# Residues of sums moved into the last attention round, a first reciprocal in two parts, and a reordered second stage, in a causal attention with a PReLU MLP behind it

## The chip, the cores and the metric

One core of one Trainium2 chip. The metric is the device time of one execution in microseconds; each kernel is timed in several runs and the median counts. "Before" has a median of 625.0 us over three runs (623.92 to 625.7).

## The reference

```python
# attention: 4 batches x 12 heads, 448 rows, 64 wide
scores = (1 / sqrt(64)) * q @ k.T                # causal mask: -1e9 above the diagonal
scores = scores - max(scores, axis=-1)
attn = exp(scores); attn = attn / (sum(attn, axis=-1) + 1e-9)
attn_out = attn @ v
x = attn_out.transpose(0, 2, 1, 3).reshape(1792, 768)
# MLP: w_in is 768 x 2048, w_out is 2048 x 768, alpha has 2048 entries
h = x @ w_in
g = maximum(h, 0) + alpha * minimum(h, 0)
out = g @ w_out
```

The MLP's weights arrive as 64-bit numbers, of which the kernel builds 32-bit ones itself.

## The kernel before, in words

**Attention.** Two heads make a pair; there are 24 pairs in 28 rounds (0 to 27). The loop `attention` runs through ORDER, a list written out by hand, once in each round; an entry such as `PT1+3` does step PT1 for the pair of three rounds ago. The letters: LK and LQ load k and q, S0, S1, S2 (SF for the first and last pair) make scores on TensorE, MX takes row maxima on VectorE, EX exponentials with their sums on ACT, RC the reciprocal of the seven sums on VectorE, NO normalizes p (on POOL; the letter behind the lag names the engine), PT transposes p on TensorE, C copies the transposes from PSUM (a is ACT, d VectorE), AV multiplies by v, XH/XN/XF/XL split the result into a rounded high part and a low part, ST stores the low parts to DRAM, LV loads chunks of v as LOADV says. Round 2 has a list of its own, SECOND_ROUND. The order of this text is the order of each engine's queue; nothing reorders it.

**Sums and residues.** The MLP's first product is done by a scheme that needs sums of the attention's results (T1 to T4, for two halves of the tokens and two column blocks: 16 in all). They lie in `spare`, the memory that later holds the accumulator acc1. Each sum becomes a rounded part (`t_hi`, line 399 on ACT or 403 on POOL) and a residue (`t_lo`, line 574), which is put into the list `late` and stored by a later `flush`. An entry `T` of the table EARLY does one sum on POOL; `th` and `tl` in the table FIRST do it on ACT and VectorE.

**Weight pieces.** A piece of the weights is loaded (LD), A (its absolute value, ACT), C (clamp, POOL), four operations D on VectorE (lines 253, 257, 260, 261), + (addition on POOL), and then cast (rounding, ACT) and sub (residue, POOL). EARLY, FRONT and REAR say in which round which piece is at which step; in a round they run at the entries ED, E2 and EA, one D at EG.

**Behind the attention.** `h_plain` makes the first group's products h = x @ w_in (24 of them, six matmuls each; 14 run inside the last rounds), with high parts from SBUF and low parts loaded back from DRAM (`load_low`, line 668, four buffers). `h_act` is the PReLU, `g_hi` and `g_lo` its rounded part and residue (lines 747, 752), `o_half` a half of a row block of the output product (six matmuls, line 786), whose bank ACT evicts for the first group (line 792). There are eight PSUM banks: four hold the h of the second token block (q = 1) until `h_act` has read it, the others and those that come free take the o halves in turn. The steps 0 to 28 of FIRST run beside these products: steps 1 to 10 behind one h product each, step 11 and later behind one o half each. In one step the kinds run in the order of KINDS: act, gh, gl, D, load, abs, cast, tl, st, th, add, S, sub, clamp. From then on four more groups follow in cycles that the change doesn't touch.

Queues: SP issues nearly all transfers and runs them in program order; a load whose data is still being stored waits there, with all behind it.

Of the kernel before, what the change touches and what calls it, by code (L numbers as in the profile page):

```python
# [24 lines left out]
EARLY = {  # L25
# [5 lines left out]
}  # L31
# [5 lines left out]
E2+4 LK+0 LQ+0 LT+4 NO00+3p NO10+3p MX11+2 NO21+3p NO11+3p EX10+2 EX11+2 MX20+2 NO20+3p MX21+2 EX20+2 NO30+3p MX00+2 EX00+2 AV+4 S2+2 LV+4 PT1+3 PT0+3 PT2+3 EX21+2 MX01+2 EX01+2 XF+4 XN+4 XH+4 C10+3a MX30+2 EG+4 XL+4 EX30+2 C00+3d C21+3d RC+2 ED+4 NO01+2p C20+3a PT3+3 S0+1 S1+1 SF+1 C30+3a EA+4 MX10+1 ST+4  # L37
# [19 lines left out]
14: D.i3.1.2 load S.S3.1 cast.A11.1  # L57
15: tl cast.S2.1
16: gh.1X gl.1X add.i3.1 sub.A11.1
17: gh.1W gl.1W cast.S3.1 sub.S2.1 S.S4.1 th  # L60
18: sub.S3.1 abs.o0.1 cast.A12.1
19: tl clamp.o0.1 sub.A12.1
20: D.o0.1.2 th
21: D.o0.1.2
22: tl add.o0.1 st load
23: gh.1Z gl.1Z abs.o1.1
24: clamp.o1.1
25: D.o1.1.1
26: D.o1.1.1
# [51 lines left out]
def kernel(  # L121
# [14 lines left out]
    nc = tc.nc  # L136
# [316 lines left out]

    def row_rec(p):
        sm, r = T["sm", p], ap["b2"].tile([P, 2 * NQ + 1], F32, tag="rs", name=f"rs_{p}")
        T["r", p] = r
        nc.vector.tensor_tensor(out=sm, in0=sm, in1=least, op=ALU.add)
        nc.vector.reciprocal(r, sm)
# [417 lines left out]
    def plan_early():  # L876
# [40 lines left out]
    low_calls = {1: 1, 2: 1, 3: 1, 4: 1, 5: 1, 7: 1, 8: 1, 9: 1, 11: 1}  # L917

    with tc.manual_schedule():
# [175 lines left out]
```

## Time and profile before

| | before |
|---|---|
| median of three runs | 625.0 us |
| profiled execution | 625.2 us |
| its span | 623.4 us |
| TensorE busy | 609.2 us (98%) |
| VectorE, POOL, ACT busy | 498.9, 397.8, 282.7 us |
| mean granted TensorE clock | 0.994 |
| attention, without its last product, until | about 171.7 us |
| second group starts | about 216 us |

The span is the time from the first to the last instruction; the execution's own time is 1.8 us longer. A granted clock of 1.00 is 2.4 GHz and 0.50 is 1.2 GHz. TensorE is busy nearly all the time, so its idle places and the places with a lower clock are where time can come from; idle time of the others costs nothing by itself. Names such as t_W are program tiles (W is one of the four blocks X, Y, Z, W of h); `<-` in brackets names the instruction that ended a wait.

### The profile page before, as it was taken

How to read it: one execution, taken by the hardware profiler on the slowest of the kernel's cores; microseconds unless marked ns; L12 is line 12 of the kernel's file. 1: busy time of each engine (PE TensorE's matmuls, PEld its weight loads, DVE VectorE, ACT ScalarE, POOL GpSimd, SP SyncE). 2: the span in 40 equal slices, each digit the busy share in tenths (PEclk: the TensorE clock that was granted, in tenths of full speed). 3: DMA queues.
4: the chain of work that ended last, by engine and by line, in shares of the span. 5: the costliest groups of instructions: out<-in, count | busy, mean ns of one | idle time of the engine just before them, and what ended most of it. 6: DMA issues, size and time to landing. Idle time of an engine off the chain costs nothing.

```text
span 623.4 us, 10906 instructions
## 1 busy us (share of the span) xinstructions
PE 609.2 (98%) x3527; PEld 532.7 (85%) x3527; DVE 498.9 (80%) x1115; ACT 282.7 (45%) x778; POOL 397.8 (64%) x531
## 2 busy tenths in 40 slices
PE   7989999999997999999999999999999999999997
PEld 4666666666877999999999999989999999999997
DVE  5889999999479678797798779868977987796364
ACT  6978989897455654232332323232333323231210
POOL 5655778767596568865776686567667766772130
PEclk9999999999998999999999999999999999999999
DMA  8674487634757479566756765685667667554725
GB/s 180 173 193 126 149 227 211 196 119 120 236 199 264 135 216 307 172 212 198 237 180 192 224 215 155 204 258 172 194 211 224 181 206 225 176 178 135 246 82 197
DMA packets 88329, 120.40 MB, mean 193 GB/s; under 512 B 12272, under 2 KB 66304, under 8 KB 88272
## 3 DMA queue, kind: packets, MB, share of 16 engines
q1 hardware_dynamic: 87664, 118.46, 61.9%
q0 software_dynamic: 288, 0.79, 0.6%
q8 instruction: 28, 0.46, 0.3%
q10 hardware_dynamic: 320, 0.46, 0.3%
q14 instruction: 29, 0.24, 0.1%
HBM read 105.00 MB, written 14.68 MB: 192 GB/s over the span
## 4 chain that ended last, share of the span: by engine, by line
PE 89%; DVE 4%; DMA 2%; POOL 1%; ACT 1%; issue 1%; SPq 1%; POOLq 0%; DVEq 0%; ACTq 0%
PE o L786 37%; PE heldY L688 11%; PE heldX L688 8%; PE a L496 6%; PE pt L477 6%; PE heldZ L688 5%; PE s L422 5%; PE s L414 3%; PE heldW L688 3%; PE h_V L688 3%; DVE s L434 1%; ACT p L449 1%; DMA low_N<-low_N 1%; DMA lo_N<-low_N 1%; PE warm L342 1%
## 5 line engine op out<-in xcount | busy, mean ns | idle before, releaser
L794 DVE TENSOR_TENSOR acc<-o,acc 128x384 f32<-128x384 f32 x196 | 107.4, 551 | 77.2 <-PE o L786 76.3
L403 POOL TENSOR_SCALAR p<-p,rs 128x128 f32<-128x128 f32 (+3 forms) x164 | 80.4, 511 | 46.6 <-ACT ptf L399 28.0
L449 ACT ACTIVATE p<-s,nm 128x256 f32<-128x256 f32 (+3 forms) x168 | 81.9, 497 | 16.1 <-DVE nm L434 15.6
L786 PE MATMUL o<-wo,g_Z 128*128 128x384 f32 x336 | 79.1, 344 | 4.2 <-DVE t_W L738 4.2
L786 PE MATMUL o<-wo,g_W 128*128 128x384 f32 x336 | 78.4, 340 | 0.3 <-POOL g_W L752 0.3
L786 PE MATMUL o<-wo,g_X 128*128 128x384 f32 x336 | 77.5, 338 | 0.0
L434 DVE CUSTOM_DVE_ANT_0 s<-s,mask 128x256 f32<-128x256 f32 (+3 forms) x168 | 70.9, 479 | 7.9 <-PE s L422 5.3
L786 PE MATMUL o<-wo,g_Y 128*128 128x384 f32 x336 | 76.9, 336 | 0.0
L786 PEld LDWEIGHTS o<-wo,g_Z 128*128 128x128 f32 x336 | 61.8, 191 | 7.6 <-ACT wi_A L291 4.5
L786 PEld LDWEIGHTS o<-wo,g_X 128*128 128x128 f32 x336 | 60.7, 188 | 3.2
L786 PEld LDWEIGHTS o<-wo,g_W 128*128 128x128 f32 x336 | 61.7, 191 | 0.6 <-POOL g_W L752 0.6
L786 PEld LDWEIGHTS o<-wo,g_Y 128*128 128x128 f32 x336 | 60.6, 188 | 0.0
L496 PEld LDWEIGHTS a<-ptf,v 128*64 128x64 f32 x384 | 25.3, 136 | 33.3 <-issue 11.8
L477 PEld LDWEIGHTS pt<-ident,p 128*128 128x128 f32 x384 | 43.1, 141 | 11.8 <-issue 7.9
L264 POOL TENSOR_TENSOR y_i<-y_i,x_i 128x384 f32<-128x384 f32 x32 | 33.5, 1047 | 27.1 <-DVE x_i L261 27.1
L496 PE MATMUL a<-ptf,v 128*64 128x448 f32 (+3 forms) x384 | 47.0, 386 | 2.2 <-DMA v<-in_v_dram 1.7
L477 PE MATMUL pt<-ident,p 128*128 128x128 f32 x384 | 47.0, 274 | 1.1 <-POOL p L403 0.7
L264 POOL TENSOR_TENSOR y_o<-y_o,x_o 128x384 f32<-128x384 f32 x32 | 32.8, 1024 | 22.4 <-DVE x_o L261 20.6
L399 ACT ACTIVATE ptf<-pt 128x512 f32<-128x512 f32 (+1 forms) x72 | 38.2, 575 | 6.5 <-PE pt L477 6.4
L247 ACT ACTIVATE x_i<-raw_i 128x384 f32<-128x384 f32 x32 | 17.8, 557 | 46.4 <-DMA raw_i<-in_moe_w_in_dram 46.4
L422 PE MATMUL s<-kr,qr 64*128 64x256 f32 (+2 forms) x288 | 38.6, 395 | 0.0
L752 POOL TENSOR_TENSOR g_Z<-t_Z,g_Z 128x384 fp32r<-128x384 f32 (+1 forms) x15 | 18.5, 1232 | 31.4 <-ACT g_Z L747 31.4
(188 smaller groups left out, 1347.0 us busy)
## 6 DMA issues: line engine op xcount, KB each, us to landing
lo_T<-low_T SPq DMA_DIRECT2D x28, 512.0 KB, 4.6
lo_B<-low_B SPq DMA_DIRECT2D x25, 512.0 KB, 4.6
raw_i<-in_moe_w_in_dram SPq DMA_DIRECT2D x32, 384.0 KB, 3.6
raw_o<-in_moe_w_out_dram SPq DMA_DIRECT2D x32, 384.0 KB, 3.6
lo_T<-low_T SPq DMA_DIRECT2D x28, 384.0 KB, 3.7
lo_B<-low_B SPq DMA_DIRECT2D x25, 384.0 KB, 3.9
lo_N<-low_N SPq DMA_DIRECT2D x16, 512.0 KB, 4.9
lo_N<-low_N SPq DMA_DIRECT2D x16, 384.0 KB, 4.6
```

Source lines behind the costliest of these rows:

```text
L264: nc.gpsimd.tensor_tensor(out=y, in0=y, in1=xf, op=ALU.add)
L399: eng.activation(out, x, AF.Copy, scale=side)
L403: eng.tensor_scalar(out=out, in0=x, scalar1=side, scalar2=1.0, op0=ALU.mult, op1=ALU.mult)
L414: nc.tensor.matmul(ps, qd[p % 3], T["k", p], start=True, stop=True)
L422: nc.tensor.matmul(ps[:, o : o + lim], T["q", p][half(j), i * QP : (i + 1) * QP], T["k", p][half(j), :lim], start=(o == 0), stop=(n > 0 or ...
L434: nc.vector.tensor_tensor_reduce(out=t, in0=t, in1=masks[1] if i == NQ else masks[0][:, (NQ - 1 - i) * QP :], scale=-SCALE, scalar=MOST_F3 ...
L449: nc.scalar.activation(T["p", p, i][:, j, : t.shape[1]], t, AF.Exp, scale=-1.0, bias=T.pop(("nm", p, i, j)), accum_out=T["sm", p][:, z : z ...
L477: nc.tensor.transpose(ps[:, j - js[0], c], t[:, j, c * QP : (c + 1) * QP], T["ident"])
L496: nc.tensor.matmul(out[half(j), c * QP :], vs[b % 2][:, hp, c, j], x[:, c * QP : S], start=(c == 0), stop=(c == NQ),)
L688: nc.tensor.matmul(ps, w[:, u, k * P : (k + 1) * P], x, start=(first and i == 0), stop=(i == len(mms) - 1), skip_group_check=True,)
L786: nc.tensor.matmul(ps[:, :NH], x, w, start=(i == 0), stop=(i == 3 * GC - 1))
L794: nc.vector.tensor_tensor(out=a[:, cols], in0=ps[:, :NH], in1=a[:, cols], op=ALU.add)
```

## The change

- EARLY: the steps of the weight pieces in rounds 5 to 19 are spread differently; what stood in round 26 goes to a new table MID, run at a new entry EH of ORDER, in front of the copies of the last transposes. In it stand seven `U`, each a sum whose rounded part is made on ACT and whose residue on VectorE, instead of four `T` on POOL. In round 26 the copy C10 goes behind EH.
- FIRST: only four sums are left there (steps 20 to 27), a flush `st` at step 0 stores the seven residues, and several steps move: h_act of block W from step 11 to 9 and of Z from 11 to 10, two of the third piece's D operations behind them, and the casts of the sums S1 to S3 one to three steps later.
- Rounds 2 and 3 have lists of their own (ROUNDS): the reciprocal of the first pair is made in two parts (RA for four sums, RB for three), its normalizations and two of its transposes move into round 2, one normalization goes to VectorE.
- `row_norm`: VectorE is used where the list asks for it, and for block 1 of the last pair alone (before: of the first and the last).
- LOADV: rounds 4 to 7 load 3, 2, 2, 0 chunks of v instead of 2, 2, 2, 1.
- Half of the first pair's q is loaded by POOL's queue instead of SP's; the memset for the warming products comes before three others.

```diff
 EARLY = {
-    5: "A:0", 6: "C:0 D:0:1", 7: "D:0:2 A:1", 8: "C:1", 12: "D:0:1 LD D:1:1 T",
-    13: "+:0 D:1:2 A:2 cast:A21", 14: "D:1:1 C:2 LD D:2:1", 15: "D:2:2 +:1 A:3 T",
-    16: "D:2:1 C:3 sub:A21 LD D:3:1 cast:A22", 17: "D:3:1 T", 18: "D:3:1 +:2 sub:A22 cast:L1", 19: "D:3:1 LD T",
+    5: "A:0", 6: "C:0 D:0:2", 7: "A:1 D:0:2", 8: "LD C:1 +:0", 9: "D:1:1 A:2", 10: "C:2", 11: "D:2:1",
+    12: "T D:1:1", 13: "D:1:2 LD cast:A21", 14: "+:1 A:3 D:2:1", 15: "D:2:1 T C:3", 16: "sub:A21 D:2:1 LD cast:A22",
+    17: "D:3:2 T", 18: "D:3:1 +:2 sub:A22 cast:L1", 19: "T D:3:1 LD",
     20: "+:3 cast:A11", 21: "sub:L1 cast:A12", 22: "sub:A11 cast:L0 A:4", 23: "sub:A12 C:4 A:5", 24: "sub:L0 C:5",
-    25: "LD +:4 T D:5:4 LD", 26: "C:6 C:7 D:6:4 LD T T +:6 T T",
+    25: "LD +:4 T D:5:4 LD", 
 }
 FRONT = {25: "D:4:4", 26: "+:5 A:6 A:7"}
+MID = {26: "C:6 C:7 U U U D:6:4 LD U U U U +:6"}
 REAR = {26: "D:7:4 LD +:7"}
-LOADV = {0: 2, 1: 2, 2: 2, 3: 1, 9: 4, 10: 3, 12: 2, 13: 3, 14: 2}
+LOADV = {0: 3, 1: 2, 2: 2, 9: 4, 10: 3, 12: 2, 13: 3, 14: 2}
...
-... C10+3a MX30+2 EG+4 XL+4 EX30+2 C00+3d C21+3d RC+2 ED+4 ...
+... C10+3a MX30+2 EG+4 XL+4 EX30+2 EH+4 C00+3d C21+3d RC+2 ED+4 ...
-SECOND_ROUND = """
-LK+0 LQ+0 MX11+2 EX10+2 EX11+2 MX20+2 MX21+2 EX20+2 MX00+2 EX00+2 EX21+2 MX01+2 EX01+2 MX30+2 S0+1 S1+1 SF+1 MX10+1 MX11+1 EX30+2 RC+2 NO01+2p
-"""
+ROUNDS = {2: """
+LK+0 LQ+0 MX11+2 EX10+2 EX11+2 MX00+2 EX00+2 MX01+2 EX01+2 MX20+2 EX20+2 MX21+2 EX21+2 RA+2 NO10+2p NO11+2p NO00+2p NO01+2p MX30+2 S0+1 S1+1 PT1+2 PT0+2 MX10+1 MX11+1 EX30+2 RB+2 NO20+2p NO21+2d NO30+2p
+""", 3: """
+LK+0 LQ+0 EX10+2 EX11+2 MX00+2 EX00+2 MX01+2 EX01+2 MX20+2 S2+2 EX20+2 MX21+2 PT2+3 EX21+2 C10+3a C00+3d MX30+2 EX30+2 C21+3d RC+2 NO01+2p C20+3a PT3+3 S0+1 S1+1 SF+1 C30+3a MX10+1
+"""}
 FIRST = """
-0: ... cast.o0.0 cast.o1.0
-1: ... cast.o2.0 cast.o3.0 th
-2: ... sub.o2.0 tl
-3: D.i1.1.2 add.i0.1 sub.o3.0 th
-4: D.i1.1.2 load tl
-5: act.1Y act.1X add.i1.1 th
-6: gh.1Y tl abs.i2.1
+0: ... cast.o0.0 cast.o1.0 st
+1: ... cast.o2.0 cast.o3.0
+2: ... sub.o2.0
+3: D.i1.1.2 add.i0.1 sub.o3.0
+4: D.i1.1.2 load
+5: act.1Y act.1X add.i1.1
+6: gh.1Y abs.i2.1
 7: gl.1Y clamp.i2.1 S.S1.1
-8: D.i2.1.2 cast.S1.1 th
-9: D.i2.1.2 load sub.S1.1 cast.L1.1
-10: add.i2.1 sub.L1.1 tl abs.i3.1
-11: act.1W act.1Z clamp.i3.1
-12: S.S2.1 cast.A22.1 th
-13: D.i3.1.2 sub.A22.1
+8: D.i2.1.2
+9: act.1W D.i2.1.1
+10: act.1Z cast.S1.1
+11: D.i2.1.1 load sub.S1.1 cast.L1.1
+12: add.i2.1 abs.i3.1 sub.L1.1
+13: clamp.i3.1 S.S2.1
...
     def load_first():
-        load(0, "q")
+        load(0, "q", also=nc.gpsimd)
...
+    def row_rec(p, cols=slice(0, 2 * NQ + 1)):
+        sm = T["sm", p]
+        if ("r", p) not in T:
+            T["r", p] = ap["b2"].tile([P, 2 * NQ + 1], F32, tag="rs", name=f"rs_{p}")
+        nc.vector.tensor_tensor(out=sm[:, cols], in0=sm[:, cols], in1=least[:, cols], op=ALU.add)
+        nc.vector.reciprocal(T["r", p][:, cols], sm[:, cols])
...
-        if p in edge and i == 1:
+        if eng is nc.vector or p == edge[1] and i == 1:
...
+        first[26] = order_of(ORDER.replace("C10+3a ", "").replace("EH+4 ", "EH+4 C10+3a "))
...
+                    elif kind == "U":
+                        fns.append(lambda: (t_hi(nc.scalar), t_lo(nc.vector)))
```

## Rows read from the trace of the kernel before

**Rows 1.** What TensorE waited for: us in total, times, longest us.

```profile
PE o L786 <- DVE t_W L738: 4.2, 1, 4.2
...
PE a L496 <- DMA v<-in_v_dram: 1.7, 1, 1.7
```

**Rows 2.** Windows of 2 us: busy us (x instructions) by engine, clock, DMA share, GB/s.

```profile
196.00:198.00 2.00, 0.00 (x0) 0.00 (x0) 1.97 (x5) 2.00 (x7) 1.83 (x3) 0.65 0.56 146
...
202.00:204.00 2.00, 2.00 (x10) 2.00 (x9) 2.00 (x2) 2.00 (x7) 2.00 (x3) 0.65 0.62 111
```

**Rows 3.** Order of time on TensorE: start us, us, instruction [idle before <-releaser].

```profile
171.74 1.95 PE L496 MATMUL a<-ptf,v 128*64 128x448 f32 x16
...
198.16 1.30 PE L786 MATMUL o<-wo,g_Z 128*128 128x384 f32 x3 [4.18 <-DVE t_W L738]
...
200.22 1.16 PE L786 MATMUL o<-wo,g_Z 128*128 128x384 f32 x3
...
201.18 1.16 PE L786 MATMUL o<-wo,g_W 128*128 128x384 f32 x3
...
204.30 0.68 PE L786 MATMUL o<-wo,g_W 128*128 128x384 f32 x3
...
204.82 0.68 PE L786 MATMUL o<-wo,g_Z 128*128 128x384 f32 x3
```

**Rows 4.** Order of time on VectorE, 165 to 199 us.

```profile
165.70 0.42 DVE L401 COPY ptf<-pt 128x256 f32<-128x256 f32 x1 [5.83 <-PE pt L477]
...
179.16 0.56 DVE L738 SCALAR_TENSOR_TENSOR t_Z<-h_Z,t_Z 128x384 f32<-128x384 f32 x1 [3.25 <-ACT t_Z L735]
...
184.38 1.44 DVE L574 TENSOR_TENSOR acc<-acc,xw 128x448 fp32r<-128x448 f32 x1
...
195.14 0.36 DVE L260 TENSOR_SCALAR x_i<-y_i 128x384 int32<-128x384 int32 x1
...
195.53 0.56 DVE L261 SCALAR_TENSOR_TENSOR x_i<-raw_i,x_i 128x384 f32<-128x384 uint32 x1
...
197.32 0.69 DVE L738 SCALAR_TENSOR_TENSOR t_W<-h_W,t_W 128x512 f32<-128x512 f32 x1
```

**Rows 5.** Residue instructions by line: ns min/median/max, first and last start us.

```profile
L574 POOL TENSOR_TENSOR acc<-acc,xw x9: 1135/1154/1330, 70.7 to 174.8; 128x448 fp32r<-128x448 f32 x9
L574 DVE TENSOR_TENSOR acc<-acc,xw x7: 612/618/1441, 184.4 to 209.8; 128x448 fp32r<-128x448 f32 x7
...
L399 ACT ACTIVATE xw<-acc x7: 560/564/570, 180.2 to 205.4; 128x448 fp32r<-128x448 f32 x7
...
L403 POOL TENSOR_SCALAR xw<-acc x9: 558/567/877, 70.1 to 173.8; 128x448 fp32r<-128x448 f32 x9
```

**Rows 6.** Order of time on ACT, behind the last transposes.

```profile
177.91 0.49 ACT L734 ACTIVATE t_Z<-h_Z 128x384 f32<-128x384 f32 x1 [2.45 <-POOL g_Y L752]
```

**Rows 7.** Order of time: SP's last store, the load behind it, its first use.

```profile
174.76 1.05 SPq L512 DMA_DIRECT2D low_N<-low_N  x2
...
179.79 0.52 SPq L668 DMA_DIRECT2D lo_N<-low_N  x1
...
185.70 0.63 PE L688 MATMUL h_W<-lo_N,wi_L 128*128 128x512 f32 x2
```

**Rows 8.** DMA: the whole kernel, and v's loads by queue (KB, us to landing).

```profile
DMA packets 88329, 120.40 MB, mean 193 GB/s; under 512 B 12272, under 2 KB 66304, under 8 KB 88272
...
v<-in_v_dram POOLq DMA_DIRECT2D x1, 336.0 KB, 5.1
...
v<-in_v_dram SPq DMA_DIRECT2D x3, 336.0 KB, 4.2
```

**Rows 9.** Order of time at the start: TensorE and ACT.

```profile
1.62 3.59 PE L342 MATMUL warm<-acc 128*128 128x512 bf16 x8 [1.62 <-DVE acc L932]
...
12.36 0.58 ACT L449 ACTIVATE p<-s,nm 128x384 f32<-128x384 f32 x1 [0.93 <-DVE nm L434]
...
16.52 1.95 PE L496 MATMUL a<-ptf,v 128*64 128x448 f32 x16 [0.50 <-ACT ptf L399]
```

More of the change, by code (lines that the diff above doesn't have):

```diff
@@ L51 @@
-8: D.i2.1.2 cast.S1.1 th
-9: D.i2.1.2 load sub.S1.1 cast.L1.1
-10: add.i2.1 sub.L1.1 tl abs.i3.1
-11: act.1W act.1Z clamp.i3.1
-12: S.S2.1 cast.A22.1 th
-13: D.i3.1.2 sub.A22.1
[L57 to L63, printed above, removed]
-21: D.o0.1.2
[L65 to L69, printed above, removed]
@@ L70 @@
-27: D.o1.1.2 load
-28: add.o1.1
+ROUNDS = {2: """
[3 more added lines that the diff above has]
+"""}
+FIRST = """
+0: gh.0Y gh.0X gl.0Y gl.0X abs.i0.1 clamp.i0.1 cast.o0.0 cast.o1.0 st
@@ new lines @@
+1: act.0Z gh.0W gl.0W D.i0.1.2 sub.o0.0 sub.o1.0 cast.o2.0 cast.o3.0
+2: gh.0Z gl.0Z D.i0.1.2 load abs.i1.1 clamp.i1.1 sub.o2.0
+3: D.i1.1.2 add.i0.1 sub.o3.0
+4: D.i1.1.2 load
+5: act.1Y act.1X add.i1.1
+6: gh.1Y abs.i2.1
+7: gl.1Y clamp.i2.1 S.S1.1
+8: D.i2.1.2
[4 more added lines that the diff above has]
+13: clamp.i3.1 S.S2.1
+14: D.i3.1.2 cast.A22.1
+15: D.i3.1.2 load sub.A22.1 S.S3.1
+16: gh.1X gl.1X add.i3.1 cast.A11.1
+17: gh.1W gl.1W cast.S2.1 sub.A11.1 S.S4.1
@@ L72 @@
+18: cast.S3.1 sub.S2.1 abs.o0.1
+19: sub.S3.1 cast.A12.1 clamp.o0.1
+20: sub.A12.1 D.o0.1.2 th
+21: D.o0.1.2
+22: tl add.o0.1
+23: gh.1Z gl.1Z load abs.o1.1 th
+24: clamp.o1.1 tl
+25: D.o1.1.1 th
+26: D.o1.1.1 tl th
+27: D.o1.1.2 tl
+28: load st add.o1.1
 """
@@ L347, in half, with load @@
         return slice(j * D, (j + 1) * D)
-    def load(p, nm, eng=nc.sync):
+    def load(p, nm, eng=nc.sync, also=None):
         b, hp = pairs[p]
@@ L355, in load @@
         for j in range(2):
-            eng.dma_start(out=T[nm, p][half(j)], in_=src[:, j, :w])
+            (also if j and also else eng).dma_start(out=T[nm, p][half(j)], in_=src[:, j, :w])
         if nm == "q":
@@ L452, in row_exp @@
         )
[L454 to L458, printed above, removed]
+    def row_rec(p, cols=slice(0, 2 * NQ + 1)):
[4 more added lines that the diff above has]
+        nc.vector.reciprocal(T["r", p][:, cols], sm[:, cols])
     def row_norm(p, i, j, eng):
@@ L583 @@
     steps = {
-        "LV": load_v_next, "RC": row_rec, "AV": av, "XH": x_hi, "XN": x_hi_plain, "XF": x_sums, "XL": x_lo, "ST": lambda p: flush(stores),
+        "LV": load_v_next, "RC": row_rec, "RA": lambda p: row_rec(p, slice(0, 4)), "RB": lambda p: row_rec(p, slice(4, 2 * NQ + 1)), "AV": av, "XH": x_hi, "XN": x_hi_plain, "XF": x_sums, "XL": x_lo, "ST": lambda p: flush(stores),
     }
-    plan, front, behind_it, gap = {}, {}, {}, {}
+    plan, front, behind_it, gap, mid = {}, {}, {}, {}, {}
     choice = {}
@@ L608 @@
     steps["ED"] = lambda p: [fn() for fn in plan.pop(p + 4, ())]
+    steps["EH"] = lambda p: [fn() for fn in mid.pop(p + 4, ())]
     steps["EG"] = lambda p: [fn() for fn in gap.pop(p + 4, ())]
@@ L625, in attention @@
     def attention(hooks):
-        order, second = order_of(ORDER), order_of(SECOND_ROUND)
+        order, first = order_of(ORDER), {n: order_of(x) for n, x in ROUNDS.items()}
+        first[26] = order_of(ORDER.replace("C10+3a ", "").replace("EH+4 ", "EH+4 C10+3a "))
         last = max(lag for lag, *_ in order)
         for n in range(len(pairs) + last):
-            for lag, name, fn in second if n == 2 else order:
-                if (n, name) == (3, "MX11"):
-                    continue
+            for lag, name, fn in first.get(n, order):
                 if 0 <= n - lag < len(pairs):
@@ L879, in name_of @@
             return f"i{i}" if i < 4 else f"o{i - 4}"
-        for table, to in ((EARLY, plan), (FRONT, front), (REAR, behind_it)):
+        for table, to in ((EARLY, plan), (FRONT, front), (MID, mid), (REAR, behind_it)):
             for n, todo in table.items():
@@ L894, in plan_early @@
                         fns.append(load_next)
+                    elif kind == "ST":
+                        fns.append(lambda: flush(late))
+                    elif kind == "U":
+                        fns.append(lambda: (t_hi(nc.scalar), t_lo(nc.vector)))
                     elif kind == "T":
@@ L917 @@
     low_calls = {1: 1, 2: 1, 3: 1, 4: 1, 5: 1, 7: 1, 8: 1, 9: 1, 11: 1}
+    v_loads = (x for b in range(B) for x in load_v(b))
     with tc.manual_schedule():
@@ L923 @@
         open_pools(att_a, "right", {"mk": 1, "v0": 1, "in": 3})
+        warm_sb = spare[:, :256].bitcast(BF16)
+        nc.vector.memset(warm_sb, 0.0)
         for n in range(3):
@@ L930 @@
         load_first()
-        warm_sb = spare[:, :256].bitcast(BF16)
-        nc.vector.memset(warm_sb, 0.0)
         open_pools(att_b, "left", {"low": 3, "v1": 1, "p3": 1, "pt": 2, "b2": 2, "b4": 8, "p": 2})
@@ L954 @@
         plan_early()
-        v_loads = (x for b in range(B) for x in load_v(b))
         after(1, "LQ", load_v_some, 4)
```

5 lines of the change are left out of this document (1 added, 4 removed).

## The prediction

> **What bounds the kernel now.** I read the time in the 40 slices first: TensorE is busy nearly throughout and its clock is full everywhere but in one slice, so only the few places where it stands can give anything. The list of what TensorE waited for [rows 1] names two that matter: 4.2 us in the output products of the second half, once, put down to VectorE's activation of h_W, and 1.7 us in the attention, once, for a load of v. Windows of 2 us around the first [rows 2] show no TensorE work in 196 to 198, and a clock of 0.65 there and again in 202 to 204, with half speed (1.2 GHz) between. 0.65 is a mixture of 1.0 and 0.5, so the low level lasted from about 196.6 to 203.4. The order of time on TensorE [rows 3] gives the price. The product that waits starts at 198.16, so the engine stood from 193.98. While the clock is low, groups of three products follow each other at 0.96 us (200.22, 201.18), at full clock at 0.52 us (204.30, 204.82). The 5.2 us from 198.16 to 203.4 would thus take 2.8 us: 2.4 us lost. The whole hole costs 4.2 + 2.4 = 6.6 us.
>
> Then I asked why VectorE is late there [rows 4]. It stands 5.83 us before 165.70 (waiting for the last transposes) and 3.25 us before 179.16, and in between and after it is full: its first subtraction for a residue takes 1.44 us at 184.38, and h_W of the second block is done only at 197.32 + 0.69 = 198.0. TensorE needed the bank at 193.98, so VectorE is 4.0 us late; h_Z, needed one half product later, is late by about as much.
>
> **The change part by part.** *Residues.* Sixteen are made: before, nine wholly on POOL (four of them in round 26) and seven behind the attention, rounded on ACT and subtracted on VectorE. After, POOL makes five, round 26 makes seven on ACT and VectorE, and four come late (steps 20 to 27). A pair costs 0.57 + 1.15 us on POOL, 0.56 us on ACT, and 0.62 us (median; 1.44 at worst) on VectorE [rows 5]. In round 26 ACT pays 7 x 0.56 = 3.9 us while it waits for the transposes anyway. VectorE pays 7 x 0.62 = 4.3 us, plus one weight piece's four operations (about 2 x (0.36 + 0.56) = 1.8 us) that move up with them: 6.1 us. Its idle time begins at 165.70 - 5.83 = 159.9 [rows 4]; behind ACT's first rounding it starts at about 160.4 and ends at 166.5, so the two copies that stood at 165.70 come 0.8 us late and end at about 167.5. They are needed by the last product with v at 171.74 [rows 3], 4.2 us later, and h_plain products cover it: cost nothing. At the worst rate, 7 x 1.44 = 10.1 us, the cover is gone (the slower rival below). I take 0.62, since POOL, whose four pairs leave this very stretch, has only two clamps and one addition there.
>
> What the moves give h_W on VectorE: (a) the 3.25 us idle before 179.16, which came about because ACT could not get a tile for t_Z until POOL had made the residue of g_Y, 2.45 us late [rows 6]; that stood behind two of POOL's pairs, 2 x 1.72 = 3.4 us, and they are gone. (b) Four subtractions ahead of h_W in VectorE's queue, 1.44 + 3 x 0.62 = 3.3 us. (c) h_W moves from step 11 to step 9, so that two operations of the third piece (0.36 + 0.56 us, at 195.14 and 195.53 [rows 4]) pass behind it: 0.9 us. Together at most 7.5 us where 4.0 are needed. Not all of it arrives: the pieces still wait for POOL's clamps, and POOL is full from g_Y on. Replaying the three queues in program order with these durations I get h_W done at about 192.5, 1.5 us ahead of need, and h_Z about 1 us ahead. The roundings of the sums, one to three steps later, no longer stop ACT ahead of the evictions of o. So the hole closes: 6.6 us, and the clock has no cause to fall. Bounds: 0 to 6.6.
>
> *What can be late next.* VectorE is full from 176 on, and at 6.6 us less time for TensorE the next thing needed from it is the residue of g_X of the second block; my replay brings it up to 1 us late. I charge 0.5 us. The second is a transfer. The stores of the seven residues now stand in SP's queue right behind the last low_N, which is issued at 174.76, and ahead of the load lo_N, issued at 179.79 once that store has landed and first used at 185.70 [rows 7]. Seven issues at about half of 1.05 us are 3.7 us and fit into those 5 us. But 7 x 224 KB = 1.6 MB then go ahead of the load: at the kernel's mean of 193 GB/s [rows 8] that is 8.1 us, at worst up to 183.9, so that the load would be late by 0 to 4.1 us, of which the slack between its usual landing and 185.70 swallows some. The piece loads that shared this stretch have moved up. I charge 0.5 us. The hole is worth 6.6 - 0.5 - 0.5 = 5.6 us.
>
> *v.* The last chunk for the second batch is issued in round 7, in the round before its first use, and TensorE waits 1.7 us for it [rows 1]. After, rounds 4 to 6 issue all seven (3, 2, 2), so it comes a whole round earlier. The one more issue in round 4 costs SP about half a us, beside prefetches of a round's lead. VectorE and ACT both idle in that wait, and TensorE sets the pace of the rounds behind it, so all 1.7 us should stay. Bounds 0 to 1.7.
>
> *Start.* The warming products follow a memset that now comes before three others, about 0.4 us earlier; they run from 1.62 for 3.59 us [rows 9], and the scores follow at once. The reciprocal in two parts and the transposes pulled into round 2 let the first pair's normalization begin behind four exponentials instead of seven; two normalizations leave VectorE (one comes), and with them ACT's idle 0.93 us for the second pair's maxima at 12.36 should shrink. The first product with v starts at 16.52, having waited 0.50 us for ACT's copies: ACT's chain of 14 exponentials and 4 copies sets that time, so it gains at most 0.93 + 0.4 = 1.3 us. Against it: half of the first q now comes by POOL's queue. Before, a 336 KB load of v took 5.1 us from issue to landing by that queue and 4.2 by SP's [rows 8]; issued at about 0.75 it lands at 5.85 at the latest, 0.6 us after the warming ends at 5.21. Bounds -0.6 to +1.3; I take +0.7, nearer to ACT's row, since the 96 KB of q are a fraction of that load.
>
> The Trainium skill, "SBUF — State Buffer", section "SBUF: two separate sides", speaks against this edit: a transfer issued from POOL has its descriptors written by POOL, and these wait while VectorE holds the shared port, so it can land far later than its size says. By the rule the start would lose about 0.6 us instead of gaining 0.7. The 0.9 us between the two queues agrees with a dearer start by POOL, but shows no such blocking.
>
> *The rest.* Pieces A, C, D of rounds 5 to 19 are spread more evenly, no round gets more than one VectorE operation (about 0.5 us) beyond its old count, and TensorE sets the pace there: nothing, with 0.2 us a round for half a dozen rounds as the worst. The four late residues need 4 x 0.62 on VectorE in steps 20 to 27, where seven stood spread before: nothing.
>
> **Sum**: 0.7 + 1.7 + 5.6 = 8.0 us. The profiled execution took 625.2 us (span 623.4 and 1.8 around it), 0.2 above the median of 625.0; 625.2 - 8.0 = 617.2 us.
>
> **Rivals.** (1) *The hole closes only in part*: the load lo_N or g_X stops TensorE for 3 to 4 us, enough to bring some of the low clock back. For it: VectorE and POOL are both full there. Against: the margins above. 617.2 + 3.3 = 620.5 us. (2) *The start loses*: the q half by POOL's queue comes late and 0.7 turns into -0.6: 618.5 us. For it the 5.1 us; against it the small size. (3) *It doesn't do what it says*: h_W stays late because POOL's clamps and additions, not VectorE's queue, set it; the hole keeps its 6.6 us, and most of v and start are all: about 623.5 us. Against it the 4.0 us needed out of 7.5. (4) *Slower*: the seven subtractions on VectorE run at 1.44 us, beside POOL, and the piece's four as much slower (2.3 times). They end at 160.4 + 10.1 + 1.8 x 2.3 = 174.6, the two copies at 175.6. The last product with v, due at 171.74, waits 3.9 us, about as long as the hole's 4.2, so I add its 2.4 us of low clock; and VectorE is so late that h_W's hole stays as well. 625.2 + 3.9 + 2.4 - 2.4 (v and start) = 629.1 us. It decides from the point where these copies end after 171.74, 4.2 us behind my replay. For it the 1.44; against it POOL's nearly empty stretch.
>
> That slow rate is what the same section of the Trainium skill states as a lock: VectorE with two inputs from SBUF and POOL exclude each other for whole instructions. This trace agrees, 0.62 us as the median against 1.44 us at 184.38 beside POOL's subtractions; since it counts only where POOL runs, it supports the low price in round 26.
>
> **How the numbers follow.** Forecast 0.60, (1) 0.17, (2) 0.10, (3) 0.07, (4) 0.06. The forecast's own range is 615.2 to 619.0. About 0.3% (1.9 us) is what a measurement of this kernel can tell from no change. Faster by more: the forecast, (1) and (2), 0.87; within: (3), 0.07; slower: (4), 0.06. The range 615.2 to 621.8 leaves out (3), (4), a little of (1) and a 0.05 for a start and hole at their best.
>
> **What would show it.** Right: no wait of TensorE over 1 us behind the attention, granted clock 1.00 in every window up to 210, h_W's bank free before it is wanted, no wait for v, the first product with v at about 15.8. Wrong: a low clock anywhere between 165 and 210; TensorE waiting for lo_N or g_X; subtractions of residues in round 26 over 1 us; the first scores after 5.3.

## The result, and the profile after

The changed kernel takes 618.0 us (median of four runs, 617.75 to 618.55) against 625.35 us: ratio 0.9882, interval 0.9854 to 0.9910, 7.3 us less by the medians. 617.2 us was forecast. The profiled execution took 617.75 us, its span is 616.0 us (before 623.4), and its mean granted clock 0.999 (before 0.994).

What TensorE waited for in the kernel after (us in total, times, longest us), to be read beside [rows 1]:

```profile
PE warm L345 <- DVE acc L933: 1.2, 1, 1.2
PE pt L480 <- POOL p L405: 0.8, 1, 0.8
PE o L789 <- DVE g_X L755: 0.5, 1, 0.5
PE s L424 <- DMA kr<-in_k_dram: 0.5, 1, 0.5
PE heldY L691 <- DMA lo_T<-low_T: 0.4, 1, 0.4
```

Both waits that the prediction named are gone, the one for h_W's activation (4.2 us) and the one for v (1.7 us). Behind the attention two small ones are new: g_X, which was foreseen, and lo_T, which wasn't. The wait for k (kr) belongs to the first scores and comes up again with the start. The clock no longer falls; windows of the stretch that held the low clock [rows 2], same columns:

```profile
196.00:198.00 2.00, 2.00 (x12) 1.68 (x10) 1.97 (x4) 0.85 (x3) 1.22 (x2) 1.00 0.09 20
198.00:200.00 2.00, 1.48 (x8) 1.48 (x9) 2.00 (x3) 2.00 (x6) 2.00 (x2) 1.00 0.53 181
202.00:204.00 2.00, 2.00 (x13) 2.00 (x12) 1.90 (x5) 2.00 (x6) 0.27 (x1) 1.00 0.00 0
```

TensorE in order of time, after: the last product with v, the output half that used to stand, the wait for g_X, the start of the second group, and its wait for lo_T. Each group of three o products takes 0.52 us from start to start, the pace of the full clock in [rows 3].

```profile
169.18 1.95 PE L499 MATMUL a<-ptf,v 128*64 128x448 f32 x16
...
191.25 0.68 PE L789 MATMUL o<-wo,g_Z 128*128 128x384 f32 x3
191.77 0.68 PE L789 MATMUL o<-wo,g_W 128*128 128x384 f32 x3
...
198.52 0.45 PE L789 MATMUL o<-wo,g_X 128*128 128x384 f32 x1 [0.52 <-DVE g_X L755]
...
207.31 0.87 PE L691 MATMUL heldX<-xw,wi_A 128*128 128x384 f32 x4
...
215.96 0.61 PE L691 MATMUL heldY<-lo_T,wi_S 128*128 128x384 f32 x2 [0.40 <-DMA lo_T<-low_T]
```

Where the 7.4 us of span went, by starts of the same instruction in both traces: the last product with v is 2.56 us earlier (171.74 to 169.18); the second group's product on heldX starts at 207.31 where it started at 215.96, another 6.09 us; from there to the end of TensorE's last product the kernel after takes 0.80 us longer, 0.40 of them by the wait for lo_T; and what lies behind the last product is 0.45 us longer. 2.56 + 6.09 - 0.80 - 0.45 = 7.4.

VectorE after, answering [rows 4]: the residues of round 26, the copies that follow them, the two activations of the first token block, then h_W and h_Z of the second and the residue of g_X.

```profile
158.09 1.70 DVE L577 TENSOR_TENSOR acc<-acc,xw 128x448 fp32r<-128x448 f32 x3 [0.79 <-ACT xw L401]
...
161.56 3.04 DVE L577 TENSOR_TENSOR acc<-acc,xw 128x448 fp32r<-128x448 f32 x4
164.51 0.88 DVE L403 COPY ptf<-pt 128x256 f32<-128x256 f32 x2
...
173.24 0.56 DVE L741 SCALAR_TENSOR_TENSOR t_Z<-h_Z,t_Z 128x384 f32<-128x384 f32 x1 [0.32 <-ACT t_Z L738]
...
188.80 0.69 DVE L741 SCALAR_TENSOR_TENSOR t_W<-h_W,t_W 128x512 f32<-128x512 f32 x1
...
190.45 0.69 DVE L741 SCALAR_TENSOR_TENSOR t_Z<-h_Z,t_Z 128x512 f32<-128x512 f32 x1
...
192.73 0.67 DVE L272 TENSOR_TENSOR S<-S,y_i 128x256 f32<-128x256 f32 x1 [1.13 <-POOL y_i L267]
194.23 0.89 DVE L256 TENSOR_SCALAR x_i<-x_i 128x384 int32<-128x384 int32 x1 [0.83 <-POOL x_i L253]
...
196.95 1.51 DVE L755 TENSOR_TENSOR g_X<-t_X,g_X 128x512 fp32r<-128x512 f32 x1
```

Three things are to be seen. The wait for t_Z of the first block, 3.25 us before, is 0.32 us. h_W is read out at 188.80 + 0.69 = 189.5, 1.8 us ahead of the half that needs its bank (191.25), h_Z at 191.1, 1.2 us ahead of the next half (192.29). And between h_Z and g_X VectorE stands 1.13 + 0.83 us for POOL; that makes g_X late. SP after, answering [rows 7]:

```profile
170.49 2.33 SPq L515 DMA_DIRECT2D low_N<-low_N  x2
172.87 4.32 SPq L515 DMA_DIRECT2D low_T<-acc  x7
177.28 0.54 SPq L671 DMA_DIRECT2D lo_N<-low_N  x1
...
204.63 3.99 SPq L515 DMA_DIRECT2D low_T<-acc  x3
209.21 0.33 SPq L234 DMA_DIRECT2D raw_o<-in_moe_w_out_dram  x1
209.69 0.32 SPq L515 DMA_DIRECT2D low_T<-acc  x1
210.07 0.52 SPq L671 DMA_DIRECT2D lo_T<-low_T  x1
```

The seven residue stores take 4.32 us of issue, and the load lo_N behind them costs nothing. What was not thought of stands further down: the four late stores and a weight piece's load are ahead of the lo_T at 210.07 that TensorE wants at 215.56 and that takes 5.9 us to land.

### The profile page after: what moved, and what is told of

It reads as the page before. It is cut to its first block, busy times and chain, and to the rows that moved or that the text cites. A ratio compares the mean times of both kernels' runs of the same rounds, so it can differ in the third digit from the quotient of the medians.

```text
span 616.0 us, 10906 instructions
## 1 busy us (share of the span) xinstructions
PE 607.5 (99%) x3527; PEld 530.5 (86%) x3527; DVE 498.5 (81%) x1120; ACT 285.2 (46%) x782; POOL 391.2 (64%) x525
## 4 chain that ended last, share of the span: by engine, by line
PE 91%; DVE 3%; DMA 2%; ACT 1%; issue 1%; POOL 1%; POOLq 0%; ACTq 0%; SPq 0%; DVEq 0%
PE o L789 35%; PE heldY L691 11%; PE heldX L691 8%; PE a L499 7%; PE pt L480 6%; PE heldZ L691 6%; PE s L424 5%; PE s L416 3%; PE h_V L691 3%; PE heldW L691 3%; PE h_Y L691 1%; PE h_W L691 1%; PE h_X L691 1%; PE h_Z L691 1%; DMA lo_T<-low_T 1%; ACT p L451 1%
## 5 line engine op out<-in xcount | busy, mean ns | idle before, releaser
L405 POOL TENSOR_SCALAR p<-p,rs 128x128 f32<-128x128 f32 (+3 forms) x165 | 82.2, 520 | 42.2 <-ACT ptf L401 27.1
L436 DVE CUSTOM_DVE_ANT_0 s<-s,mask 128x128 f32<-128x128 f32 (+3 forms) x168 | 71.2, 480 | 9.0 <-PE s L424 5.3
L789 PE MATMUL o<-wo,g_Z 128*128 128x384 f32 x336 | 77.5, 338 | 0.0
L424 PE MATMUL s<-kr,qr 64*128 64x384 f32 (+2 forms) x288 | 39.5, 395 | 0.7 <-DMA kr<-in_k_dram 0.5
L250 ACT ACTIVATE x_i<-raw_i 128x384 f32<-128x384 f32 x32 | 17.8, 556 | 42.6 <-DMA raw_i<-in_moe_w_in_dram 42.6
```

The lines of the kernel that those rows point to most:

```text
L405: eng.tensor_scalar(out=out, in0=x, scalar1=side, scalar2=1.0, op0=ALU.mult, op1=ALU.mult)
L424: nc.tensor.matmul(ps[:, o : o + lim], T["q", p][half(j), i * QP : (i + 1) * QP], T["k", p][half(j), :lim], start=(o == 0), stop=(n > 0 or ...
L436: nc.vector.tensor_tensor_reduce(out=t, in0=t, in1=masks[1] if i == NQ else masks[0][:, (NQ - 1 - i) * QP :], scale=-SCALE, scalar=MOST_F3 ...
L789: nc.tensor.matmul(ps[:, :NH], x, w, start=(i == 0), stop=(i == 3 * GC - 1))
```

## The experiments

Kernels that are compared share runs of the kernel before: its medians are 624.77 us for the first four, 624.63 us for the next four and 624.99 us for the last four. Each of these three sets ran on a chip of its own. The theory was that the hole closes because VectorE's queue ahead of h_W gets shorter, by the idle time that POOL's pairs caused and by the subtractions moved away, and that v and the start add their own gain.

**v alone.** The kernel before with one line:

```diff
-LOADV = {0: 2, 1: 2, 2: 2, 3: 1, 9: 4, 10: 3, 12: 2, 13: 3, 14: 2}
+LOADV = {0: 3, 1: 2, 2: 2, 9: 4, 10: 3, 12: 2, 13: 3, 14: 2}
```

> The kernel before with the new distribution of v's chunks alone (3, 2, 2 in rounds 4 to 6). Theory: the wait of 1.66 us for v goes and stays gone, 0.2 us behind it with it: -1.9 us, no wait of TensorE for v. Rival: the transfer's place is taken by another load of the attention, since SP now issues one more in round 4: 0 us, a new wait for kr, qr or qd.

624.06 us, ratio 0.9984 [0.9971, 0.9997]: 0.7 us by the medians, 0.2 to 1.8 by the interval. The wait for v is gone from its trace and the hole is unchanged (TensorE waits 4.2 us for h_W's activation). The gain is below the 1.7 us of [rows 1] because that wait isn't the same in every execution: the profiles of kernels that load v as before show 1.7, 0.8, 0 (no such line), 1.9, 1.7, 1.6 and 0 us. These are seven kernels, which differ elsewhere, with one profile each. Their mean is 1.1 us; [rows 1] caught a long one.

**The hole alone.** The kernel before with the seven `U` in MID, C10 behind them, and the new FIRST: residues and order together.

> The kernel before with the seven residues in round 26, their stores behind the last low part and the new order of the second stage, and nothing else (start, v and the pieces of rounds 5 to 19 as before). Theory: the hole of 4.2 us and the low clock of 2.4 us go, about 0.5 us comes back for g_X and 0.8 us for late lo_T: -5.3 us, granted clock 1.00 throughout. Rival: the even spread of the pieces in rounds 5 to 19 or the earlier start has a share in it: -3 us or less, a hole of over 1 us left.

618.94 us, ratio 0.9917 [0.9901, 0.9934], 5.8 us less by the medians (4.1 to 6.2). No wait for h_W, clock 0.999, g_X 0.3 us late.

**Residues without the new order.**

```diff
+MID = {26: "C:6 C:7 U U U D:6:4 LD U U U U +:6"}
...
-8: D.i2.1.2 cast.S1.1 th
-9: D.i2.1.2 load sub.S1.1 cast.L1.1
-10: add.i2.1 sub.L1.1 tl abs.i3.1
+8: D.i2.1.2 cast.S1.1
+9: D.i2.1.2 load sub.S1.1 cast.L1.1
+10: add.i2.1 sub.L1.1 abs.i3.1
 11: act.1W act.1Z clamp.i3.1
```

> As the kernel with the hole's changes alone, but the steps of the second stage keep the old places of h_act and of the casts of the sums: only the residues move. Theory: the two terms of the residues (3.25 us idle before t_Z, four subtractions ahead of h_W, 3.3 us) are enough for the 4.0 us that h_W was late, so the hole closes to under 1 us and the clock stays up: -4.5 to -5.3 us. Rival: without h_W's earlier step and the later roundings a wait of 2 us or more stays for h_W or for an eviction behind a cast: -1 to -3 us.

617.98 us, ratio 0.9902 [0.9886, 0.9918], 6.8 us less (5.1 to 7.1). The hole closes fully with h_W at its old step: t_W ends at 191.8 there, and the half that needs its bank starts at 192.51. g_X isn't waited for either; its residue starts at 195.89. But TensorE waits 0.44 us for lo_T.

**The new order without the residues.**

```diff
-11: act.1W act.1Z clamp.i3.1
...
+9: act.1W D.i2.1.1
+10: act.1Z cast.S1.1 tl
...
```

> The kernel before with the new order of h_act and of the casts in the second stage alone; the residues stay where they were. Theory: this gives h_W 0.9 us of the 4.0, so the hole is still about 3 us and the clock still falls: -1 to -1.5 us. Rival: the roundings that stopped ACT ahead of the evictions were what mattered: the hole closes, -5 us.

625.42 us, ratio 1.0019 [1.0001, 1.0037]: no gain. The profiled execution was the longest of its twelve, 629.44 us, so its waits are not those of the median. TensorE's two long waits there:

```profile
PE o L786 <- DVE g_X L752: 3.6, 1, 3.6
PE o L786 <- DVE t_W L738: 2.7, 1, 2.7
```

The order does what it should for h_W, whose wait falls from 4.2 to 2.7 us, and the clock stays at 1.00 through that one. But what it moved behind h_W now stands in front of g_X, whose residue starts at 207.48; TensorE stands 3.62 us for it and the clock falls to 0.50 there. In this execution the wait was moved and grew, to 2.7 + 3.6 us from 4.2; the timed runs say only that the order alone gains nothing.

**The changed kernel again, with the old order, and with q by SP.** Sent together. The second takes the changed kernel and puts the steps 8 to 20 of FIRST back (and its loads one step earlier); the third has

```diff
     def load_first():
-        load(0, "q", also=nc.gpsimd)
+        load(0, "q")
```

> The changed kernel itself once more, as the measure for the others of this set: 617 to 618.5 us, with waits of 0.5 us for g_X and 0.4 us for lo_T.

> The changed kernel with the old places of h_act, of the third piece's operations and of the casts in the second stage; the residues stay in round 26. Theory: with the residues gone the new order is no longer needed for h_W, and it makes g_X late, because the third piece's last operation comes after POOL's next clamp; with the old one g_X is ready over 1 us ahead and its wait goes: 0.5 us less than the changed kernel. Rival: h_W, whose margin shrinks to under 1 us, becomes late instead: 0 to 2 us more than the changed kernel.

> The changed kernel with both halves of the first q by SP's queue again. Theory: by POOL's queue the half is issued at 1.29 and holds the third score product until 5.5, so the earlier warming gains nothing; by SP it lands about 1 us earlier, the first exponential starts at about 6.4 instead of 6.88 and the first product with v 0.4 us earlier: 0.4 us less than the changed kernel. Rival: it is k that is late, and SP's later issues then come 0.6 us later: 0 to 0.6 us more.

618.09 us (617.74 to 618.41), 616.92 us (615.86 to 617.61) and 617.83 us (617.18 to 618.5); ratios to before 0.9885 [0.9862, 0.9909], 0.9865 [0.9841, 0.9889] and 0.9881 [0.9858, 0.9905]. The old order is 1.2 us better than the new one, and the six runs of the one don't overlap with the six of the other. Its trace has neither the wait for g_X nor the one for lo_T. Its VectorE from h_W to g_X:

```profile
190.61 0.69 DVE L741 SCALAR_TENSOR_TENSOR t_W<-h_W,t_W 128x512 f32<-128x512 f32 x1
...
191.99 0.69 DVE L741 SCALAR_TENSOR_TENSOR t_Z<-h_Z,t_Z 128x512 f32<-128x512 f32 x1
192.60 0.72 DVE L272 TENSOR_TENSOR S<-S,y_i 128x256 f32<-128x256 f32 x1
193.24 0.35 DVE L256 TENSOR_SCALAR x_i<-x_i 128x384 int32<-128x384 int32 x1
...
195.42 1.50 DVE L755 TENSOR_TENSOR g_X<-t_X,g_X 128x512 fp32r<-128x512 f32 x1
```

h_W and h_Z are done 1.5 to 1.8 us later than in the kernel after, but TensorE wants them 1.4 us later too (192.65 and 193.69), so that the margins are 1.35 and 1.0 us. The two waits for POOL behind h_Z are not there: the third piece's D operations end before h_W, so POOL's addition is done when VectorE comes to it. g_X starts 1.5 us earlier. The lo_T load is issued at 209.22, not at 210.07, since its step is one earlier. That alone doesn't make it safe: the residues alone, with the same old order, issued it at 209.70 and had 0.44 us of wait, since landing took 6.9 us there, and 5.9 us in the kernel after. The q half is worth nothing that these runs show, 0.26 us between the medians with ranges that overlap.

**Stores and a load later.** The old order, and the last residues' stores and the last piece's load behind the first lo_T loads of the next group.

```diff
-22: tl add.o0.1
-23: gh.1Z gl.1Z load abs.o1.1 th
+22: add.o0.1 load tl
+23: gh.1Z gl.1Z abs.o1.1 th
...
-25: D.o1.1.1 th
+25: D.o1.1.1 th st
...
-28: load st add.o1.1
+28: add.o1.1
...
-1: cast.o0.0 abs.o2.0 clamp.o2.0
+1: load cast.o0.0 abs.o2.0 clamp.o2.0
...
-4: D.o3.0.2 add.o2.0 cast.o1.0 sub.S4.0
+4: D.o3.0.2 add.o2.0 cast.o1.0 sub.S4.0 st
...
-                    fn = lambda: (flush(late), t_lo(nc.vector))
+                    fn = lambda: t_lo(nc.vector)
```

The last line belongs to it: a `tl` no longer issues the stores that are due, only an `st` does.

> As the kernel with the old order above, and the last stores of residues and the last piece load of the second stage moved behind the first loads lo_T of the next group (SP's queue). Theory: SP stood behind these stores, which wait for VectorE, so that a lo_T came 0.4 us late and another 0.1; with them behind, both waits go: 0.7 us less than the kernel with the old order alone. Rival: the buffer of lo_T comes free no earlier, so nothing changes, or the piece that loads later makes VectorE late: 0 to 1 us more.

616.93 us, ratio 0.9866 [0.9840, 0.9892]. lo_T is issued at 208.50, another 0.7 us earlier, but the old order alone had left no wait for it in its profile: nothing to gain that the runs show.

**The four pairs alone.** The kernel before; the four `T` of round 26 become `U`, and with them the whole entry of that round moves to MID, in front of the copies of the last transposes, as in the change: the sixth piece's clamps, D operations and addition, and C10 behind them. All seven subtractions of FIRST and its order stay, four of them ahead of h_W (the expectation speaks of three: the ones that the change moves as well).

```diff
-    25: "LD +:4 T D:5:4 LD", 26: "C:6 C:7 D:6:4 LD T T +:6 T T",
+    25: "LD +:4 T D:5:4 LD",
+MID = {26: "C:6 C:7 U U D:6:4 LD U U +:6"}
```

> The kernel before with only the four residues of round 26 that GpSimd made (the pairs T) moved to ScalarE and VectorE; the three subtractions in the hole and its order of instructions stay as before. If GpSimd's pairs ahead of g_Y are what sets the hole (my theory), g_Y is made early, h_W is free of the 2.45 us that ScalarE waited for it, and TensorE's wait for t_W falls from 4.2 to about 1 us: 4 to 5 us less in all, about 620. If the three subtractions on VectorE matter as much (rival), 2 us or more of the wait stay and the gain is 1 to 3 us, 621.5 to 623.5.

620.19 us, ratio 0.9917 [0.9895, 0.9939], 4.8 us less (3.8 to 6.6). VectorE's wait, and TensorE's, in that trace:

```profile
176.80 0.56 DVE L741 SCALAR_TENSOR_TENSOR t_Z<-h_Z,t_Z 128x384 f32<-128x384 f32 x1 [0.32 <-ACT t_Z L738]
```

```profile
195.84 0.76 PE L789 MATMUL o<-wo,g_Z 128*128 128x384 f32 x3 [0.87 <-DVE t_W L741]
```

VectorE's 3.25 us become 0.32, and TensorE's 4.18 us become 0.87: 2.9 us less idle on the one is 3.3 us less wait on the other. The clock stays at 1.00. That is the theory's number, and the rival (2 us or more of wait stay) is out.

What the run doesn't separate is seen on POOL in the kernel before (L250 to L264 are a weight piece, L403 and L574 a pair):

```profile
170.72 1.06 POOL L264 TENSOR_TENSOR y_o<-y_o,x_o 128x384 f32<-128x384 f32 x1 [6.44 <-DVE x_o L261]
171.75 0.87 POOL L403 TENSOR_SCALAR xw<-acc 128x448 fp32r<-128x448 f32 x1
...
174.77 1.16 POOL L574 TENSOR_TENSOR acc<-acc,xw 128x448 fp32r<-128x448 f32 x1
...
176.86 1.02 POOL L752 TENSOR_TENSOR g_Y<-t_Y,g_Y 128x384 fp32r<-128x384 f32 x1
```

Two pairs stand ahead of g_Y and take 4.1 us (171.75 to 175.9). But they are late because the sixth piece's addition ahead of them waits 6.44 us for VectorE, whose D operations for it stood behind the copies. With the entry moved, that addition comes at 164.55, and g_Y at 172.68. The 6.44 us would have held the two pairs, so moving the piece and leaving the pairs on POOL might have freed g_Y too. No run tries that: shown is that POOL's queue ahead of g_Y made the hole, not that the pairs had to leave POOL.

**The start alone.** ROUNDS, the reciprocal in two parts, the q half by POOL's queue and the memset first, in the kernel before.

```diff
+... EX21+2 RA+2 NO10+2p NO11+2p NO00+2p NO01+2p MX30+2 S0+1 S1+1 PT1+2 PT0+2 MX10+1 MX11+1 EX30+2 RB+2 ...
-        load(0, "q")
+        load(0, "q", also=nc.gpsimd)
```

> The kernel before with the changes at the start alone: first reciprocal in two parts, half of the first q by GpSimd's queue, the memset for the warming first, and the order of rounds 2 and 3. My theory from the profile of after: first product with v 0.4 us earlier and 0.4 us less in all, about 624.2. The prediction's own sum gives 0.7 us less; the rival, that the first scores wait longer for the half of q on GpSimd's queue than the reciprocal gives back, gives 0 to 0.6 us more.

626.03 us, ratio 1.0016 [1.0000, 1.0031]: no gain, and rather a loss. Its TensorE at the start:

```profile
1.19 3.59 PE L344 MATMUL warm<-acc 128*128 128x512 bf16 x8 [1.19 <-DVE acc L926]
4.72 2.68 PE L424 MATMUL s<-kr,qr 64*128 64x256 f32 x12
...
10.64 1.49 PE L480 MATMUL pt<-ident,p 128*128 128x128 f32 x6 [0.79 <-POOL p L405]
...
13.92 2.27 PE L424 MATMUL s<-kr,qr 64*128 64x256 f32 x12
16.43 1.95 PE L499 MATMUL a<-ptf,v 128*64 128x448 f32 x16 [0.24 <-ACT ptf L401]
```

The warming starts 0.43 us earlier than in [rows 9], but the first twelve scores take 2.68 us, so that they end at 7.4; the kernel before ended them at 5.15 + 1.86 = 7.0, the one after at 7.0 (with 0.46 us of waiting for k), the one with q by SP at 6.95. The 2.68 us are not a wait. The weight loads (PEld) of these scores, here and in the kernel after, and those of the hole before, where the granted clock was 0.50 (ns: least, median, most):

```profile
L424 PEld LDWEIGHTS s<-kr,qr x12: 188/286/334, 4.7 to 6.6; 64*128 64x128 f32 x12
...
L424 PEld LDWEIGHTS s<-kr,qr x12: 182/186/188, 4.4 to 6.2; 64*128 64x128 f32 x12
...
L786 PEld LDWEIGHTS o<-wo,g_W x7: 330/330/330, 198.9 to 202.8; 128*128 128x128 f32 x7
```

So a load takes 0.33 us at 0.50, and 0.19 at 1.00. Nine of the twelve here take 0.27 to 0.33: most of these scores ran at the low level, 1.2 GHz, though the row of the granted clock reads 1.00 from the start. In five of the fourteen profiles no load of the first scores is slow and the twelve end at 6.8 to 7.1; in the other nine 2 to 12 of the twelve loads are, and they end at 7.0 to 8.7. With the change at the start the mean end is 7.46, without it 7.30: when TensorE came to its full pace, and k where that was early, set the moment, not when the warming began. The transposes do start 0.9 us earlier (10.64, 11.56 before), but the next scores take 2.27 us where 1.57 is usual, and the first product with v, at 16.43, is 0.09 us earlier. This profile accounts for no loss at the start: it is 0.2 us ahead of before at 48 us and 0.5 us behind at the last product with v, after one round that took 6.71 us instead of 6.08 (0.37 us of it a wait for low_N, a kind that other traces have too). Why the timed runs are some 1 us slower stays open; the low level at the start differs from one execution to the next and may have a share.

**The spread pieces alone**, rounds 5 to 19 of EARLY as in the change:

```diff
-    5: "A:0", 6: "C:0 D:0:1", 7: "D:0:2 A:1", 8: "C:1", 12: "D:0:1 LD D:1:1 T",
+    5: "A:0", 6: "C:0 D:0:2", 7: "A:1 D:0:2", 8: "LD C:1 +:0", 9: "D:1:1 A:2", 10: "C:2", 11: "D:2:1",
...
```

> The kernel before with the redistribution of the pieces of rounds 5 to 19 alone. My theory: no difference, within 0.3 us of before. Rival: the attention gets shorter by it, 0.3 to 0.5 us less.

624.71 us, ratio 0.9990 [0.9974, 1.0007]: no difference that can be told, as expected.

**All together that helped or cost nothing**: the changed kernel with the old order, the late stores, and q by SP.

> The kernel after with the old order of instructions in the hole, the last residue stores and the last piece's load behind the first loads of lo_T, and both halves of the first q on SP's queue. My theory: the parts add, 0.3 to 0.5 us less than the old order with late stores alone (616.9), about 616.4. Rival: no difference from it, 616.9.

616.98 us, ratio 0.9865 [0.9844, 0.9886]. No more than the old order alone gives (616.92, in another set): the rival's number. The gains don't add; in the profile of the old order the two waits that the other edits were aimed at were already gone. The simplest better kernel is thus the change with its old steps 8 to 20.

The profiles put these together. Start of the last product with v, and from there to the end of TensorE's last product (us, of one profiled execution each):

| kernel | until last v product | from there |
|---|---|---|
| before | 171.7 | 448.0 |
| v alone; start alone; spread alone | 171.5; 172.2; 171.0 | 447.5; 448.1; 448.3 |
| order alone | 173.4 | 450.6 |
| four pairs alone | 172.7 | 442.3 |
| residues alone | 170.4 | 441.9 |
| residues and order (hole alone) | 171.0 | 442.1 |
| after, twice; with q by SP | 169.2, 169.1; 169.1 | 442.7, 442.8; 442.6 |
| after with the old order; late stores; best | 170.0; 169.9; 169.9 | 441.6; 441.3; 441.3 |

The right column falls into two levels, about 448 with the hole and about 442 without, and the four pairs alone make nearly the whole step in these profiles; the timed runs give them 4.8 us where all seven residues have 6.8, with intervals that overlap. The new order costs 1.1 us of it in the changed kernel (442.7 against 441.6), in the kernel before with the residues 0.2 (442.1 against 441.9; 1.0 us by the medians). The order alone, at 450.6, is the long execution. The left column is less sharp: kernels whose attention is unchanged up to round 25 (before, order, four pairs, residues, hole) lie between 170.4 and 173.4.

## Why the prediction was right, point by point

**The hole**, forecast at 5.6 us of 6.6: right in size. The part alone gives 5.8 us by the medians. The path is shown by the four pairs alone: removing the 3.25 us of [rows 4], which the prediction traced over ScalarE to POOL's queue ahead of g_Y [rows 6], closes the hole but for 0.87 us. It put the lateness of g_Y down to two pairs, 3.4 us; they took 4.1 us, and stood late behind the sixth piece's addition, which the prediction didn't name. Its (b), the subtractions ahead of h_W, brings the rest: with the residues alone there is no wait left. Its (c), h_W two steps earlier, was not needed, nor were the later roundings of the sums: the residues alone have both in their old places. The new order to which they belong cost about 1 us. The prediction counted (c) as a gain, and charged g_X with 0.5 us without seeing that the two are one: 0.52 us were measured, and the old order has none. The replay's margins, 1.5 us for h_W and about 1 us for h_Z, came out as 1.8 and 1.2 us.

**Round 26.** VectorE's seven subtractions took 1.70 + 3.04 = 4.7 us, 4.3 forecast. The copies end at 165.4, 3.8 us ahead of the last product with v, 4.2 forecast. So the slower rival, 1.44 us each, is out. But one of the seven did take 1.43 us, which is among the prediction's own signs of being wrong, as is TensorE's wait for g_X; both stayed small. It starts at 162.1, and POOL's only addition in this stretch lies beside it:

```profile
L577 DVE TENSOR_TENSOR acc<-acc,xw x7: 610/619/1429, 158.1 to 164.0; 128x448 fp32r<-128x448 f32 x7
...
161.72 1.31 POOL L267 TENSOR_TENSOR y_o<-y_o,x_o 128x384 f32<-128x384 f32 x1 [3.54 <-DVE x_o L264]
```

The Trainium skill, "SBUF — State Buffer", section "SBUF: two separate sides", states that a VectorE instruction with two inputs from SBUF and a POOL instruction that reads SBUF lock each other out for whole instructions. This trace agrees: the one beside the addition took 1.43 us, the six others 0.61 to 0.62. The price was low since POOL was nearly idle there.

**Transfers.** The 0.5 us for lo_N behind 1.6 MB of stores was 0 in the kernel after: issued at 177.28, used at 183.13, a lead of 5.9 us as before [rows 7] (0.35 us in the kernel with the old order). In its place stood a wait that the prediction had not looked for, lo_T with 0.4 us here and 0.7 us in the second profile. That the two charges are of one size is luck. It charged the stores that it saw move to step 0 and not the four that stayed and moved to the end, ahead of the next group's first loads.

**v**, forecast at 1.7 us, is mis-sized, as far as the runs tell: 0.7 us in the timed ones (0.2 to 1.8, so that 1.7 is just inside). The profile after agrees with the forecast, as the round with the wait goes from 7.95 to 6.08 us, but a wait that is 0 to 1.9 us from one profile to the next is worth its mean, 1.1 us in seven, not the figure of one profile.

**The start**, forecast at +0.7 us, can't be confirmed: alone it gave nothing or a loss of up to 1.9 us. In seven profiles with it (two of them with q by SP) the first product with v starts at 15.99 to 16.90, against 15.8 forecast; in six of the seven others at 16.26 to 17.11, and in one, whose clock was at 0.50 around 16 us, at 18.40. The means of seven and six are 16.33 and 16.68: some 0.35 us that the spread of either, 0.9 us, covers. The step that failed is "and the scores follow at once", which makes the scores earlier by the earlier warming: they end at 7.0 in the profiles before and after, and at 6.8 to 8.7 in all, by when TensorE leaves the low level and when k arrives. The rival there, that POOL's queue makes the q half late, isn't the cause either: the half is issued at 1.29 and takes 3.6 us to landing, so it is there at 4.9; by SP, in the kernel before, the second half was issued at 1.40 and took 4.0 us, to 5.4.

```profile
qr<-in_q_dram POOLq DMA_DIRECT2D x1, 96.0 KB, 3.6
```

By the rule of the Trainium skill that spoke against this edit (the same section) the load could have come far later. No run here shows that; VectorE has only memsets in this stretch, to 1.57, and then nothing until 6.35.

**The sum.** v and the start came out below their 2.4 us when each was tried alone (0.7 us won, 1.0 us lost, and 0.3 us by the spread that can't be told from nothing). All attention edits together are worth 0.85 us (618.94 to 618.09, across two sets of runs) or 1.06 us (617.98 to 616.92). The hole came out 0.2 us above its term, and 5.8 + 0.85 = 6.65 us agrees with the 6.5 us of the changed kernel's second set (624.63 to 618.09). Against the 8.0 us of the sum, 1.5 us are missing, and by these medians they lie in the two small terms. That 617.2 us was only 0.8 us too low is in part luck: it was counted down from 625.2 us, and the kernel before has 624.6 to 625.0 in its larger sets. By the time alone the rival in which the start loses (618.5 us) is nearer than the forecast; its sign fits the start alone (a loss of 0 to 1.9 us), its cause doesn't.

## What to carry to other kernels

When TensorE waits for an engine, look for the last stretch in which that engine itself stood, and for what stopped it: here two steps back, POOL's queue ahead of the residue of g_Y holding ScalarE's tile, and freeing it was worth 4.8 of the 5.8 us. Then ask why that queue was late itself, and move one thing at a time. An instruction that is put earlier than needed in one queue puts others later, so its margin is checked together with the next consumer's; the margin that the new order added here was of no use and cost a us elsewhere. A wait read from one profile for a transfer that varies is priced by several profiles, and parts that each remove a wait are not added up before it is seen that they remove different ones.

## What the runs showed of the hardware that was not expected

The same wait of 4.2 us cost the clock differently from one profile to the next. With v alone, the granted clock was still 1.00 while TensorE stood, and fell only when it had restarted:

```profile
196.00:198.00 2.00, 0.12 (x1) 0.15 (x2) 1.97 (x4) 1.87 (x5) 2.00 (x3) 1.00 0.71 220
198.00:200.00 2.00, 2.00 (x7) 2.00 (x8) 1.93 (x5) 0.51 (x3) 1.19 (x3) 0.53 0.83 229
200.00:202.00 2.00, 2.00 (x9) 2.00 (x9) 1.93 (x5) 2.00 (x5) 0.59 (x1) 0.62 0.41 150
```

The low level holds there for (1.00 - 0.53) x 4 + (1.00 - 0.62) x 4 = 3.4 us, in the kernel before for 6.8 us, from the standing on [rows 2], and as long in the profiles of the start alone and of the spread alone, which have the same wait. So the 2.4 us that the prediction added for the clock can be about 1.7 us too (half of 3.4). With the order alone TensorE stood 2.67 us with the clock at 1.00 in all windows behind it, and some us later 3.62 us, behind which it ran at 0.50. And the row of the granted clock does not show the low level at the start: the first scores of the start alone take 0.33 us for a weight load, as at 0.50 in the hole, under a row that reads 1.00.
